# A long-convolution kernel on one Trainium2 core: giving K and X of the product stage PSUM tiles of their own, shared by two units

## The chip, the core and the metric

The kernel runs on one core of a Trainium2 chip. The engines that matter are PE (TensorE, matmuls; its weight loads are shown as PEld), DVE (VectorE), ACT (ScalarE), POOL (GpSimd) and SP, which issues DMAs. The metric is the device time of one execution in microseconds (us).

## The reference

Two blocks follow each other on a sequence of S = 2048 tokens of D = 512 channels. The first is a gated long convolution of `k` and `v`, the second a dense layer with ReLU.

```python
k_shift = sum over t of k_pad[:, t:t+S, :] * shift_k[:, ks-1-t]      # ks = 4 taps
kv  = k_shift * v
y   = irfft(rfft(kv padded to 2S) * rfft(ssm_k padded to 2S))[:S]    # per channel
y   = y + kv * ssm_D
h   = x + layernorm(x) * y                                           # x = A_q
out = h + relu(layernorm(h) @ w1) @ w2
```

The product of the two spectra is what the changed part computes.

## The kernel before, in words

The Fourier transform is done with matmuls in two steps, and so is its inverse. Stage 1 (line 312) transforms the convolution kernel `ssm_k` into the tile BK and the sequence `kv` into the tile BX. BK and BX hold 32 values of a first frequency index, called k1 below, for all 512 channels. The **product stage** (lines 444 to 524) makes the second transform step for each k1 and multiplies the two spectra. Inverse step 1 (line 610, tiles `psi`) follows, then for each quarter of the tokens inverse step 2 (line 701, `pz`), the gate (line 687) and the two matmuls of the dense layer (lines 713 and 729).

The product stage works in eight chunks of four k1. Each chunk has six **units**: u0 to u3, one for each k1 (weights from the table `st`), and s0 and s1, each for two k1 (weights from the table `smc`, which holds sums and differences that give the product by three real multiplications). A unit needs K (from BK) and X (from BX). The four matmuls of one **step** are two for each of two row halves (partitions 0 to 63 and 64 to 127); the halves run at the same time on the two halves of the PE array, so they come in concurrent pairs. A step has 256 columns. For u units K is a step and X is a step. In s units both halves add into the same PSUM banks, so K and X take two steps each (way 1 and way 2): way 1 has the halves write different banks, way 2 swaps the banks, and before way 2 PE waits until its own way 1 has ended (the `nop` with the added dependency, line 484).

PSUM has eight banks. `bank2` (line 151) takes a tile of two banks of 512 words, so four tiles exist at a time (pool `psF`, `bufs=4`). A new tile gets the buffer that was freed first in program order. In the kernel before, a unit has one tile: the first 256 words of each bank hold K, the second 256 hold X. `forms` (line 449) lets ACT copy the K half (2 x 256 words) to SBUF, into `ktu` or `kts`, two buffers each. `times` (line 501) lets DVE multiply X, read from PSUM, by that copy. The product of a u unit overwrites BK at its k1; that of an s unit goes into BXs, the first 32 columns of BX's tile, behind what is still to be read.

The engines run their instructions in the order in which the program has them. For the product stage this order is written out by hand in two strings, FIRST for the first chunk and OTHER for the rest (lines 506 and 507). In them `u0K` is the K step of u0, `s0X2` the second X step of s0, `+u0` an early copy of K, and `=u0` the product, with the copy ahead of it if it wasn't made early:

```python
FIRST = "u0K +u0 u1K +u1 s0K1 s0X1 u0X s0K2 =u0 u1X =u1 s0X2 =s0 s1K1 s1X1 u3K s1K2 s1X2 =s1 u2K u3X =u3 u2X =u2"
OTHER = "s0K1 s0X1 u0K u0X s0K2 u1K =u0 s0X2 =s0 s1K1 s1X1 u1X =u1 s1K2 s1X2 =s1 u3K u3X u2K =u3 u2X =u2"
```

After each chunk POOL makes the table for the chunk three later (`sum_tables`, line 409), and after three of them it adds rows of `w1` (`add_chunks`, line 442) for the column means (line 533), two tiles `pm` of four matmuls in all, which follow the stage on PE. After the stage `w1` is centered by DVE (line 596), ACT copies the second `pm` tile (line 633), POOL and SP begin the work on `x`, and inverse step 1 begins with two `psi` tiles.

Of the kernel before, what the change touches and what calls it, by code (L numbers as in the profile page):

```python
# [9 lines left out]
ALU = mybir.AluOpType  # L10
BF16 = mybir.dt.bfloat16
F32 = mybir.dt.float32
# [3 lines left out]
P = 128  # L16
# [40 lines left out]
def kernel(  # L57
# [13 lines left out]
    nc = tc.nc  # L71
# [9 lines left out]
    halves = (lo, hi)  # L81
# [9 lines left out]
    early = pl.push("early", side="right")  # L91
# [5 lines left out]
    BK = bkp.tile([P, 2, 32, 32, DC * 2], F32R, tag="K", name="BK")  # L97
# [53 lines left out]
    def bank2(name):  # L151
        return psum.tile([P, 2, 512], F32, tag="ps", name=name)[:]
# [69 lines left out]
    st = stp.tile([P, 32, 192], F32R, name="st")  # L222
# [178 lines left out]
    smc = skp.tile([P, 3, 2, 4, P], F32R, name="smc")  # L401
# [3 lines left out]
    def sum_tables(c):  # L405
        ks = slice(4 * c, 4 * c + 4)
        for dp, pq in enumerate(halves):
            for i, op in ((0, ALU.subtract), (1, ALU.add)):
                nc.gpsimd.tensor_tensor(out=smc[pq, c % 3, i, :, 64 * dp:64 * dp + 64], in0=st[pq, ks, 64:128].bitcast(F32),  # L409
                                        in1=st[pq, ks, 0:64].bitcast(F32), op=op)  # L410
# [12 lines left out]
    BX = BXt[:, :, 2:66, :].rearrange("p g (i k) x -> p i g k x", i=2)  # L423
    BXs = BXt[:, :, 0:32, :]
# [7 lines left out]
    prod = pl.push("prod", side="right")  # L432
# [7 lines left out]
    def add_chunks(step):  # L440
        o, a, b = ((wsum, w1[:, 0, :], w1[:, 1, :]), (wpair, w1[:, 2, :], w1[:, 3, :]), (wsum, wsum.bitcast(F32), wpair.bitcast(F32)))[step]
        nc.gpsimd.tensor_tensor(out=o, in0=a, in1=b, op=ALU.add)

    def cols(B, pq, k1, i):
        return B[pq, i].rearrange("p (u w) (v s) x -> p u w v (s x)", w=2, s=2)[:, :, k1 % 2, k1 // 2, :]

    def forms(ps, tag):
        kt = prod.tile([P, 2, 256], F32, tag=tag, name=tag, bufs=2)
        nc.scalar.copy(out=kt[:], in_=ps)  # L449
        return kt  # L450


    def pairs(k1):

        ps = bank2("u")
        begun = []

        def do(what):
            x = "KX".index(what[0])
            for i in range(2):  # L460
                t = st[:, k1, 64:192] if i == 0 else st[:, k1, 0:128]
                for dp, pq in enumerate(halves):
                    nc.tensor.matmul(out=ps[:, dp, 256 * x:256 * x + 256], lhsT=t[pq], rhs=cols((BK, BX)[x], pq, k1, i),  # L463
                                     start=not begun, stop=(i == 1), tile_position=(64 * dp, 0), skip_group_check=True)
                begun.append(i)
        return do, ps, "ktu", BK[:, :, :, k1, :]

    def sums(k1):

        ps = bank2("us")  # L470
        begun = []
        ways = {}

        def do(what):
            x, way = "KX".index(what[0]), int(what[1])
            last = {}
            for i in range(2):
                for dp, pq in enumerate(halves):
                    k = k1 + (dp + way - 1) % 2
                    if i == 0 and dp == 0 and (3 - way, dp) in ways:  # L480

                        turn = nc.tensor.nop()
                        for d in range(2):
                            tc.add_manual_dep(turn.ins, ways[3 - way, d], mybir.DependencyInfo(mybir.DependencyClass.Sync, mybir.DependencyReason.DATA))
                    mm = nc.tensor.matmul(out=ps[:, k % 2, 256 * x:256 * x + 256], lhsT=smc[pq, k // 4 % 3, i, k % 4, :],  # L485
                                     rhs=cols((BK, BX)[x], pq, k, i), start=not begun, stop=(i == 1 and what in begun),
                                     tile_position=(64 * dp, 0), skip_group_check=True)
                    last[dp] = mm.ins.name
                begun.extend((what[0] + "12"[2 - way], i))
            for dp in range(2):  # L490
                ways[way, dp] = last[dp]
        return do, ps, "kts", BXs[:, :, k1:k1 + 2, :].rearrange("p g k x -> p k g x")

    def copy_k(unit):
        do, ps, tag, o = unit
        return forms(ps[:, :, 0:256], tag)

    def times(unit, kt=None):
        do, ps, tag, o = unit
        kt = copy_k(unit) if kt is None else kt  # L500
        nc.vector.tensor_tensor(out=o, in0=ps[:, :, 256:512].rearrange("p b (g x) -> p b g x", x=8),  # L501
                                in1=kt[:].rearrange("p b (g x) -> p b g x", x=8), op=ALU.mult)

    FIRST = "u0K +u0 u1K +u1 s0K1 s0X1 u0X s0K2 =u0 u1X =u1 s0X2 =s0 s1K1 s1X1 u3K s1K2 s1X2 =s1 u2K u3X =u3 u2X =u2"
    OTHER = "s0K1 s0X1 u0K u0X s0K2 u1K =u0 s0X2 =s0 s1K1 s1X1 u1X =u1 s1K2 s1X2 =s1 u3K u3X u2K =u3 u2X =u2"
    for c in range(8):
        units, early = {}, {}
        for step in (OTHER if c else FIRST).split():  # L510
            if step[0] == "+":
                early[step[1:]] = copy_k(units[step[1:]])
                continue
            if step[0] == "=":
                times(units[step[1:]], early.pop(step[1:], None))
                continue
            u = step[:2]
            if u not in units:
                units[u] = (pairs if u[0] == "u" else sums)(4 * c + (1 if u[0] == "u" else 2) * int(u[1]))
            units[u][0](step[2:])  # L520
        if c + 3 < 8:
            sum_tables(c + 3)
        if c in (2, 4, 5):
            add_chunks(max(c - 3, 0))
# [28 lines left out]
    st = late.tile([P, 4, 6], F32, name="st")  # L553
# [260 lines left out]
```

## Time and profile before

| what | value |
|---|---|
| median of 3 runs | 205.06 us (204.96 to 205.13) |
| the profiled execution | 205.23 us; its span, first to last instruction, 203.1 us |
| mean granted clock of TensorE | 0.997 |
| PE busy | 194.7 us, 96% of the span |
| DVE, ACT, POOL busy | 140.3, 115.1, 79.3 us |
| product stage, first matmul to first column mean | 47.63 to 82.43 us |
| one copy of K at line 449, 512 columns | 0.59 us (median) |
| one product at line 501, 512 columns | 0.68 us (median) |

The profile page gives the busy time of each engine, the span in 40 slices, the DMA queues, the chain of work that ended last, and groups of instructions by line. The trace behind it can be asked for the waits of each engine, for busy time in stretches of time, and for the instructions in order of time. PE is busy nearly all of the span, but a busy PE is not one that works at its peak: a matmul whose weights come late is recorded as a longer matmul.

### The profile page before, as it was taken

Reading aid. Unit: us, or ns where it says so; the run is one execution under the profiler, and the core shown is the slowest. Engines: PE = TensorE matmul, PEld = TensorE weight load, DVE = VectorE, ACT = ScalarE, POOL = GpSimd, SP = SyncE. Lnnn points to the kernel's source line nnn. Section 1 sums busy time; section 2 is a strip of 40 time slices with the busy share of each in tenths; the row PEclk is TensorE's granted clock in tenths of the full one; section 3 lists DMA queues with packets and bytes.
Section 4 is the critical chain, followed back from the end, with each engine's and each line's share of the span. In section 5 each row is a group of like instructions: output and inputs, shape, how many; then the busy total and the mean of one; then the engine's idle time right before and its main releaser. Section 6 shows DMA issues by size and latency. Waiting matters only on the chain.

```text
span 203.1 us, 4751 instructions
## 1 busy us (share of the span) xinstructions
PE 194.7 (96%) x1929; PEld 136.9 (67%) x1929; DVE 140.3 (69%) x252; ACT 115.1 (57%) x198; POOL 79.3 (39%) x127
## 2 busy tenths in 40 slices
PE   8899899999999999999999999999999999999991
PEld 2565556988899999899998744475445744444460
DVE  4999988796899989997561968994298560360130
ACT  4986785898688777685980188206930174036200
POOL 7979998960569994302003032062002200002000
PEclk9999999999999999999999999999999999999998
DMA  5999990003400000151736999999734705110011
GB/s 190 330 181 226 170 163 3 3 5 91 190 3 0 3 3 0 46 135 29 107 102 203 183 210 213 177 154 94 88 65 97 138 13 103 35 57 14 0 52 52
DMA packets 47300, 19.94 MB, mean 98 GB/s; under 512 B 42186, under 2 KB 45744, under 8 KB 47280
## 3 DMA queue, kind: packets, MB, share of 16 engines
q1 hardware_dynamic: 43616, 16.14, 41.9%
q10 hardware_dynamic: 3664, 3.51, 6.0%
q8 instruction: 15, 0.25, 0.6%
q14 instruction: 5, 0.04, 0.1%
HBM read 7.02 MB, written 2.10 MB: 45 GB/s over the span
## 4 chain that ended last, share of the span: by engine, by line
PE 73%; DVE 1%; ACT 0%; issue 0%
PE ps1m L713 19%; PE ps2m L729 19%; PE psi L610 11%; PE us L485 9%; PE pz L701 7%; PE u L463 7%; PE pm L533 1%; DVE BX L280 0%; DVE BX L501 0%; ACT kts L449 0%; DVE M L731 0%; DVE ax L280 0%
## 5 line engine op out<-in xcount | busy, mean ns | idle before, releaser
L715 ACT ACTIVATE M<-ps1m 128x512 bf16<-128x512 f32 (+1 forms) x44 | 25.1, 595 | 49.4 <-PE ps1m L713 39.0
L729 PE MATMUL ps2m<-M 128*128 128x512 bf16 (+3 forms) x187 | 38.7, 366 | 0.0
L729 PEld LDWEIGHTS <-M 128*128 128x128 bf16 (+1 forms) x187 | 18.2, 98 | 19.9
L713 PEld LDWEIGHTS <-w 128*128 128x128 bf16 (+1 forms) x176 | 17.4, 100 | 19.9
L572 POOL TENSOR_SCALAR rstd<-mv 128x4 f32<-128x4 f32 x8 | 2.2, 276 | 70.2 <-DVE mv L570 70.2
L409 POOL TENSOR_TENSOR smc<-st 64x256 fp32r<-64x256 f32 x32 | 22.8, 731 | 11.2 <-PE us L485 10.3
L731 DVE SCALAR_TENSOR_TENSOR M<-ps2m,rstd,M 128x512 bf16<-128x512 f32 (+1 forms) x13 | 9.2, 707 | 24.2 <-PE ps2m L729 15.7
L501 DVE TENSOR_TENSOR BK<-u,ktu 128x512 fp32r<-128x512 f32 x32 | 21.2, 685 | 3.8 <-ACT ktu L449 3.5
L610 PE MATMUL psi<-inv,BK 128*128 128x128 f32 x128 | 21.1, 255 | 0.0
L449 ACT COPY ktu<-u 128x512 f32<-128x512 f32 x32 | 18.1, 600 | 5.3 <-PE u L463 4.4
L610 PE MATMUL psi<-inv,BX 128*128 128x256 f32 x64 | 20.5, 338 | 0.0
L610 PEld LDWEIGHTS psi<-inv,BK 128*128 128x128 f32 x128 | 19.7, 197 | 0.0
L713 PE MATMUL ps1m<-M,w 128*128 128x512 bf16 (+1 forms) x88 | 19.3, 379 | 0.0
L713 PE MATMUL ps1m<-xT,w 128*128 128x512 bf16 (+1 forms) x88 | 19.3, 379 | 0.0
L485 PE MATMUL us<-BK,smc 64*128 64x256 f32 x128 | 14.4, 300 | 0.4 <-DVE BX L280 0.4
L463 PE MATMUL u<-BK,st 64*128 64x256 f32 x128 | 13.6, 290 | 0.3 <-DVE BX L501 0.2
L485 PE MATMUL us<-BX,smc 64*128 64x256 f32 x128 | 13.3, 281 | 0.0
L463 PE MATMUL u<-BX,st 64*128 64x256 f32 x128 | 13.1, 283 | 0.0
L278 ACT CAST BK<-ps 128x512 fp32r<-128x512 f32 x16 | 9.1, 587 | 6.4 <-PE ps L312 4.4
L610 PEld LDWEIGHTS psi<-inv,BX 128*128 128x128 f32 x64 | 12.1, 196 | 0.3 <-DVE BK L501 0.3
L568 DVE BATCH_NORM_STATS2 st<-M 128x6 f32<-128x512 bf16 x20 | 12.3, 677 | 0.0
L687 DVE TENSOR_TENSOR qT<-pz,qT 128x2048 bf16<-128x2048 f32 x2 | 4.6, 2290 | 10.6 <-DMA qT<-M 6.5
(132 smaller groups left out, 411.6 us busy)
## 6 DMA issues: line engine op xcount, KB each, us to landing
E<-in_A_ssm_k_dram SPq DMA_DIRECT2D x1, 2048.0 KB
out_dram<-M ACTq DMA_DIRECT2D x15, 128.0 KB
w<-in_B_w_dram SPq DMA_DIRECT2D x1, 1376.0 KB
M<-in_B_w_dram ACTq DMA_DIRECT2D x1, 1280.0 KB
M<-in_A_q_dram SPq DMA_DIRECT2D x8, 128.0 KB
xh<-in_A_q_dram SPq DMA_DIRECT2D x4, 128.0 KB
xr<-in_A_q_dram SPq DMA_DIRECT2D x4, 128.0 KB
out_dram<-M ACTq DMA_DIRECT2D x2, 64.0 KB
```

Of the source, the lines that this page charges most:

```text
L409: nc.gpsimd.tensor_tensor(out=smc[pq, c % 3, i, :, 64 * dp:64 * dp + 64], in0=st[pq, ks, 64:128].bitcast(F32), in1=st[pq, ks, 0:64].bitcas ...
L449: nc.scalar.copy(out=kt[:], in_=ps)
L463: nc.tensor.matmul(out=ps[:, dp, 256 * x:256 * x + 256], lhsT=t[pq], rhs=cols((BK, BX)[x], pq, k1, i), start=not begun, stop=(i == 1), til ...
L485: mm = nc.tensor.matmul(out=ps[:, k % 2, 256 * x:256 * x + 256], lhsT=smc[pq, k // 4 % 3, i, k % 4, :], rhs=cols((BK, BX)[x], pq, k, i), s ...
L501: nc.vector.tensor_tensor(out=o, in0=ps[:, :, 256:512].rearrange("p b (g x) -> p b g x", x=8), in1=kt[:].rearrange("p b (g x) -> p b g x", ...
L568: nc.vector.bn_stats(out=st[:, i, :], in_=src[:, i, :])
L610: nc.tensor.matmul(out=o if part == 0 else o[:, P * part - P:P * part], lhsT=src[:, g // 2, :, g % 2::2].rearrange("p c r -> p (c r)"), rh ...
L701: nc.tensor.matmul(out=pz[:, i, :, a:a + w, :].rearrange("p (s r) a n -> p s r (a n)", s=2), lhsT=ax[rho][:, n2 // 2, n2 % 2, :], rhs=ecor ...
L713: nc.tensor.matmul(out=ps1[:fsz, :].rearrange("p (i t) -> p i t", i=4), lhsT=w1[:, c, fc * P:fc * P + fsz], rhs=hT[sc][:, :, c, :], start= ...
L715: nc.scalar.activation(out=h1T[:fsz, fc, :], in_=ps1[:fsz, :], func=ACT.Relu)
L729: nc.tensor.matmul(out=ps2, lhsT=h1T[:ksz, fc, i * P:(i + 1) * P], rhs=w2[:ksz, fc, d0:d0 + w], start=(fc == 0), stop=(fc == NFC - 1))
L731: nc.vector.scalar_tensor_tensor(out=o[:, d0:d0 + w], in0=ps2, scalar=rstd2[:, t, :], in1=xh[sc][:, i, d0:d0 + w], op0=ALU.mult, op1=ALU.add)
```

## The change

K and X get PSUM tiles of their own, each of two banks, and each shared by two units: u0 and u1 share a K tile and an X tile, u2 and u3 do, and s0 and s1 do. A chunk still takes six tiles from the pool. In a tile the results of the two units (or, for s, of the two k1 of a bank) are interleaved: runs of 8 words of the one, then of the other, so that a product can read its tile, and write BK or BXs, in longer runs. ACT copies a whole K tile (1024 columns, three buffers of one tag `kt`), and DVE multiplies a whole X tile (1024 columns). s units now pair the k1 differently: step `s0` covers the first k1 of each of the two banks, `s1` the second. PE's wait for itself comes once for K and once for X of a chunk, where the kernel before has it for each s unit. The order strings change: K of u0 and u1 of the next chunk (marked `'`) and its copy come ahead of the last X steps and the last product of a chunk, and the first chunk begins with six K steps.

```diff
-    def pairs(k1):
-        ps = bank2("u")
...
-    def sums(k1):
-        ps = bank2("us")
...
+    tiles = {}
+
+    def step(c, what):
+        x, e = "KX".index(what[2]), int(what[1])
+        key = c, what[0] + str(e // 2), x
+        if key not in tiles:
+            tiles[key] = bank2(what[0] + what[2]), set(), {}
+        ps, begun, ways = tiles[key]
+        pv = ps.rearrange("p b (u s k x) -> p b k u s x", s=2, k=2, x=8)
+        way = int(what[3]) if what[0] == "s" else 1
+        if 3 - way in ways:
+            turn = nc.tensor.nop()
+            for mm in ways.pop(3 - way):
+                tc.add_manual_dep(turn.ins, mm, mybir.DependencyInfo(mybir.DependencyClass.Sync, mybir.DependencyReason.DATA))
+        last = {}
+        for i in range(2):
+            for dp, pq in enumerate(halves):
+                if what[0] == "u":
+                    bank, k = dp, 4 * c + e
+                    t = st[pq, k, 64:192] if i == 0 else st[pq, k, 0:128]
+                else:
+                    bank = (dp + way - 1) % 2
+                    k = 4 * c + e + 2 * bank
+                    t = smc[pq, c % 3, i, k % 4, :]
+                mm = nc.tensor.matmul(out=pv[:, bank, e % 2], lhsT=t, rhs=cols((BK, BX)[x], pq, k, i), start=bank not in begun,
+                                      stop=(i == 1), tile_position=(64 * dp, 0), skip_group_check=True)
+                begun.add(bank)
+                last[dp] = mm.ins.name
+        if what[0] == "s":
+            ways.setdefault(way, []).extend(last.values())
+
+    def copy_k(c, name):
+        kt = prod.tile([P, 2, 512], F32, tag="kt", name="kt", bufs=3)
+        nc.scalar.copy(out=kt[:], in_=tiles[c, name, 0][0])
+        return kt
+
+    def times(c, name, kt):
+        ps = tiles[c, name, 1][0]
+        if name[0] == "u":
+            k = 4 * c + 2 * int(name[1])
+            o = BK[:, :, :, k:k + 2, :].rearrange("p d g k x -> p d g (k x)")
+        else:
+            o = BXs[:, :, 4 * c:4 * c + 4, :].rearrange("p g (b k) x -> p b g (k x)", b=2)
+        nc.vector.tensor_tensor(out=o, in0=ps.rearrange("p b (g y) -> p b g y", y=16), in1=kt[:].rearrange("p b (g y) -> p b g y", y=16), op=ALU.mult)
...
-    FIRST = "u0K +u0 u1K +u1 s0K1 s0X1 u0X s0K2 =u0 u1X =u1 s0X2 =s0 s1K1 s1X1 u3K s1K2 s1X2 =s1 u2K u3X =u3 u2X =u2"
-    OTHER = "s0K1 s0X1 u0K u0X s0K2 u1K =u0 s0X2 =s0 s1K1 s1X1 u1X =u1 s1K2 s1X2 =s1 u3K u3X u2K =u3 u2X =u2"
+    FIRST = "s0K1 s1K1 u0K u1K +u0 s0K2 s1K2 +s0 u0X u1X =u0 s0X1 s1X1 u2K u3K +u1 s0X2 s1X2 =s0 u0K' u1K' +u0' u2X u3X =u1"
+    OTHER = "s0K1 s1K1 u0X u1X s0K2 s1K2 +s0 =u0 s0X1 s1X1 u2K u3K +u1 s0X2 s1X2 =s0 u0K' u1K' +u0' u2X u3X =u1"
```

In the new strings `+u0` and `=u0` stand for the pair u0 and u1, `+u1` and `=u1` for the pair u2 and u3, and `+s0` and `=s0` for both s units. In the prediction a tile is called by its letters, so sK is the K tile of the s units of a chunk, and uK' is the K tile of the next chunk's u0 and u1.

## The prediction

> **What bounds the kernel now.** I read the page first, then the waits and the busy time by stretches of the product stage (47.6 to 84.1 us), then its timeline, since the stage is the only one that the change touches. The page's first part gives each engine's busy time, its share of the span and its instructions; the group rows give busy time and mean ns, then the idle time before and who ended it.
>
> ```profile
> PE 194.7 (96%) x1929; PEld 136.9 (67%) x1929; DVE 140.3 (69%) x252; ACT 115.1 (57%) x198; POOL 79.3 (39%) x127
> L501 DVE TENSOR_TENSOR BK<-u,ktu 128x512 fp32r<-128x512 f32 x32 | 21.2, 685 | 3.8 <-ACT ktu L449 3.5
> ```
>
> TensorE is the bound, and the waits view gives it only 0.2 us of idle time after 84 us: what the product stage ends earlier, the kernel ends earlier. The stage runs from its first matmul (47.63) to the first of the column means (82.43). The stretches below are its first chunk, one in the middle and the last (stretch, length, then busy us of PE, PEld, DVE, ACT, POOL):
>
> ```profile
> 47.63:52.55 4.92, 4.51 (x66) 4.24 (x66) 2.94 (x5) 3.27 (x8) 0.54 (x1) 1.00 0.75 246
> 61.34:65.56 4.22, 4.22 (x66) 4.04 (x65) 3.86 (x7) 3.32 (x7) 4.07 (x4) 1.00 0.00 0
> 78.23:82.43 4.20, 4.20 (x66) 4.03 (x65) 3.86 (x7) 3.30 (x7) 0.04 (x1) 1.00 0.00 0
> ```
>
> PE looks full, but "busy" hides stalls here, because matmuls overlap and one that waits for its weights is recorded as longer. The starts of the steps (four matmuls each, 16 steps a chunk) tell more:
>
> ```profile
> 60.97 0.41 PE L463 MATMUL u<-BX,st 64*128 64x256 f32 x4
> 61.11 0.68 DVE L501 TENSOR_TENSOR BX<-us,kts 128x512 fp32r<-128x512 f32 x1
> 61.34 0.51 PE L485 MATMUL us<-BK,smc 64*128 64x256 f32 x4
> ...
> 61.90 0.46 PE L463 MATMUL u<-BK,st 64*128 64x256 f32 x4
> ...
> 62.19 0.41 PE L463 MATMUL u<-BX,st 64*128 64x256 f32 x4
> ...
> 62.65 0.59 ACT L449 COPY ktu<-u 128x512 f32<-128x512 f32 x1 [0.61 <-PE u L463]
> 62.68 0.41 PE L463 MATMUL u<-BK,st 64*128 64x256 f32 x4
> ```
>
> Undisturbed steps start 0.242 us apart (62.19 and 62.68 have one step between them), 0.121 per pair of concurrent matmuls. Sixteen would take 3.87; a chunk takes 4.22. The missing 0.35 is at the chunk's first step (60.97 to 61.34, a tile that a product still reads), at the next unit (61.90 to 62.19, the same, released by the product that ends at 61.79) and at s1K2 (0.1, TensorE's wait for its own s1X1 one step earlier). DVE has 3.86 busy of 4.22: PE and DVE nearly pace each other. Over the stage: 128 steps x 0.242 = 31.0 of its 34.8 us; 3.8 us are stalls, 1.05 in the first chunk (4.92 - 3.87), 0.69 in the second (4.56, same view), 0.35 in each of the other six.
>
> **The change part by part.** *Matmuls:* the same 512, same weights and moving operands; 30.98 us stay. *Copies:* 48 of 512 columns become 24 of 1024; *products* likewise. The trace has both sizes from PSUM:
>
> ```profile
> L295 ACT COPY xfl<-pst 128x1024 f32<-128x1024 f32 x2 | 2.0, 1024 | 0.7 <-PE pst L291 0.7
> L350 DVE TENSOR_TENSOR E<-pkv,E 128x1024 bf16<-128x1024 f32 x6 | 7.3, 1220 | 1.3 <-PE pkv L347 1.3
> ```
>
> ACT per chunk: 3 x 1.02 = 3.06 instead of 6 x 0.59 (the copy at 62.65) = 3.54. DVE: queued products of 512 start 0.60 apart (two take 1.28 at 82.80, so 1.28 - 0.68), those of 1024 then 0.60 + (1.220 - 0.685) = 1.13; 3 x 1.13 = 3.4 instead of 6 x 0.60 = 3.6. Neither reaches 3.87, so neither is the pace by itself. What counts is which tile comes free late.
>
> *Waits on tiles.* The buffer that was freed first in program order goes to the next tile; the changed program's waits agree. In a steady chunk, counted in pairs (0.121) from its first: sK (pair 0) takes the tile freed by the last chunk's copy +u1, uX (pair 4) that of product =s0, sX (pair 12) that of copy +u0', uK (16) that of =u1, the next uK' (24) that of +s0, uX (28) that of =u0. A step whose last pair starts at j releases its reader 0.28 (one matmul) + 0.04 later (62.60 to 62.65 above). A released PE goes on 0.16 after the product's end: 61.79, and the step after the waiting one at 62.19 instead of 0.242 after its start, so 62.19 - 0.24 - 61.79.
> - =s0: s1X2's last pair is 23, so 2.78 + 0.32 = 3.10; + 1.22 = 4.32; PE may go on at 4.48. The next uX is due at pair 36, 4.36. **Stall 0.12 to 0.14.** As a loop from uX to the next uX: 19 pairs 2.30 + 0.32 + 1.22 + 0.16 = **4.00 us a chunk**, against 4.22.
> - +u1: u3K's last pair 19: 2.30 + 0.32 + 1.02 = 3.64; its semaphore about 0.05 later; the weights of sK are due one pair ahead of it, at 3.75. Slack 0.06, and a loss up to 0.14 beyond it costs nothing, as uX waits right behind.
> - +s0: 1.33 + 0.32 + 1.02 = 2.67; uK' is due at 2.78: slack 0.06. =u0 starts at 1.65 (it may overwrite BK only after s1K2), ends 2.87; due 3.27. =u1 starts 1.13 behind =s0, at 4.23, ends 5.45, which is 1.45 in the next chunk; due 1.82. +u0' ends 4.60, due 5.2.
> - TensorE's own wait before s0K2 and s0X2 now has two steps between: its 0.1 a chunk goes.
>
> *First chunk.* Now it stalls for the last copies of the stage before (chain of waits, start and length):
>
> ```profile
> 48.09 0.61 DVE BX L280
> 48.70 0.14 issue
> 48.83 0.75 PE us L485 x8
> ```
>
> Two steps had run since 47.63, so 48.83 was due at 48.11: 0.7 lost. Afterwards six K steps come before the first that needs BX or these tiles: 47.63 + 6 x 0.242 = 49.08, behind the end of the copies (48.70 on DVE, about 48.82 on ACT). What hides them is the moved K work; nothing is late in its place, since +u0 (48.8 to 49.8) and +s0 (to 50.8) meet their tiles at 49.9 and 50.9, with 0.05 each.
>
> *Tail.* What follows hangs on the last product's end:
>
> ```profile
> 82.80 1.28 DVE L501 TENSOR_TENSOR BK<-u,ktu 128x512 fp32r<-128x512 f32 x2
> ...
> 83.53 1.36 PE L610 MATMUL psi<-inv,BX 128*128 128x256 f32 x8
> 83.99 3.08 DVE L596 TENSOR_TENSOR w<-w,pm 128x1376 bf16<-128x1376 bf16 x2
> ```
>
> It ends at 84.08, and the second psi tile, the centering, the copy of pm, POOL's and SP's first loads of x all start within 0.15 us of it. A product of 1024 makes this tail worse: =u1 has to queue behind =s0.
>
> *Sum.* First uX of chunk 1: =s0 of the first chunk is released by pair 27: 3.27 + 0.32 + 1.22 + 0.16 = 4.97, so 52.60. Six loops of 4.00: 76.60. Last =s0 starts at 76.60 + 2.30 + 0.32 = 79.22, =u1 1.13 later, 80.35, and ends at 81.57. That is 2.5 us ahead of 84.08 (the stalls and products saved give about 2.9, the tail takes 0.4 back). One 0.05 us semaphore instruction on PE and a few near-zero slacks take some: **2.4 us**. POOL is no bound: its table and column sums follow chunk 2 as now and end some 1.2 us sooner than today's 78.3, before the column means at about 79.5. No DMA is added or moved; w1 is issued at 47.63 as now. The profiled execution took 205.23 (span 203.1 and 2.1 around it); 205.23 - 2.4 = 202.8. The runs shown have the median 205.06, so **202.7** in their terms.
>
> *One cost that the trace doesn't show:* results are now written in runs of 8 words with gaps of 8. Nearest row: the stage-1 matmuls (L312) write 128 columns in four runs of 32, and their pairs start 0.055 apart (46.16, 46.22, 46.27 in the timeline). The MLP's matmuls take 9.51 us for 44 of 512 columns, 0.00042 a column, so 128 need 0.054: at most 0.001 for four runs, below 0.0005 a gap (or nothing). 256 columns need 0.108, and the pace here is 0.121 (psi at L610 shows why: there 128 columns take 0.114 each, 16 from 84.73 to 86.56, and 256 take 0.12, so the weights are the limit), so 31 gaps of 0.0005 make 0.124 at most: 0.8 us over the stage if nothing hides it. I take 0, the value of the nearest row, and keep 0.8 for the range. The Trainium skill speaks against the change: PSUM — Partial Sum Buffer, Specifications (TRN2), has 8-byte cachelines there and says that "any non-contiguous AP slows matmuls significantly". It gives no price. By that sentence the sum above would be too low; L312's rows do not agree with it for runs of 32, and no run here shows runs of 8.
>
> **Rivals.**
> - *The product paces more than its row says* (partial gain). For: the loop of 4.00 holds one product in full, and each 0.1 on it costs 7 x 0.1. Against: 512-column products keep to 678 to 693 ns with POOL busy beside them. At 1.40 instead of 1.22: 1.3 us less gain, 204.0.
> - *Gaps cost time, slower.* Price if a run takes as long as the 16 words that it spans: 512 x 0.00042 = 0.215 a pair, 256 x 0.215 = 55.0 instead of 34.8, and 0.4 for the tail: 225.7. It decides from about 0.132 a pair (32 pairs then take today's 4.22), or 0.0008 a gap. Against: L312.
> - *It doesn't do what it says:* K a group ahead brings nothing, because today PE waits for products, not copies. Then only the head and TensorE's own wait are gained (0.7 + 8 x 0.1), the tile waits of today come back elsewhere, and the longer tail (0.4) and the uX stall (0.14 x 7) eat it: 205.0. Against: the waits above, of which only uX comes late.
>
> **How the numbers follow.** Forecast (201.8 to 203.6) 0.73; product paces 0.13; no effect 0.05; gaps 0.09. A measurement of this kernel tells about 0.2% (0.4 us) from no change. Low end: no uX stall at all, another 0.9 gained, 201.8. High end: the 0.8 of the gaps and half of the first rival, 204.2; gaps beyond that and the rest are left out. Faster: 0.73 + 0.12 + 0.01 = 0.86; same 0.04; slower 0.10.
>
> **What would show it.** Right: chunks of 4.00 +- 0.05 us; a stall of uX on the 1024 product and nowhere else above 0.05; no wait between 47.63 and the first uX; products at 1.22 and copies at 1.02; steps 0.242 apart; last product ending 81.4 to 81.9; the rest as long as now. Wrong: steps further apart (gaps), chunks of 4.2 with a longer product, or PE idle time behind 84 us that is not there today.

## The result and the profile after

| what | before | after |
|---|---|---|
| median | 205.09 us (204.91 to 205.20, 6 runs) | 203.01 us (202.78 to 203.68, 6 runs) |
| the profiled execution, and its span | 205.23, 203.1 | 203.68, 201.9 |
| first matmul of the product stage | 47.63 | 48.07 |
| end of the last product, from there | 36.45 | 34.82 |
| end of the last product to the end of the span | 119.0 | 119.0 |

The changed kernel takes 0.9897 of the time before, with an interval of 0.9876 to 0.9919. That is 2.08 us less, where 2.4 were forecast. The product stage accounts for 1.63 of it in the traces, not for 2.5. The page's busy times and its groups for the product, in the columns of the page shown before:

```profile
PE 193.6 (96%) x1921; PEld 136.3 (68%) x1929; DVE 138.0 (68%) x228; ACT 112.5 (56%) x174; POOL 79.4 (39%) x127
L494 DVE TENSOR_TENSOR BK<-uX,kt 128x1024 fp32r<-128x1024 f32 x16 | 19.5, 1219 | 3.2 <-PE sK L475 1.9
L494 DVE TENSOR_TENSOR BX<-sX,kt 128x1024 fp32r<-128x1024 f32 x8 | 9.8, 1224 | 1.9 <-PE sX L475 1.9
```

A product of 1024 columns takes what the row of the same size took in the kernel before (1220 ns). The next view gives the busy time by stretches of the stage; the chunks are the first, the second and one in the middle:

```profile
48.07:52.53 4.46, 4.46 (x73) 4.46 (x74) 2.97 (x4) 4.33 (x7) 0.80 (x2) 1.00 0.73 230
52.53:56.60 4.07, 4.07 (x68) 3.95 (x66) 3.54 (x4) 2.96 (x4) 2.84 (x5) 1.00 0.25 98
64.83:68.94 4.11, 4.11 (x68) 3.96 (x66) 3.58 (x4) 2.96 (x4) 3.96 (x6) 1.00 0.02 4
```

The first chunk has 18 steps now (two of the next chunk's), which need 4.36 at 0.242 each: of 1.05 us of stalls 0.10 are left. A steady chunk takes 4.07 to 4.12 instead of 4.22; 4.00 were forecast. The timeline around one uX step tells where the 0.1 is (start, length, operation, idle time before and its releaser):

```profile
63.38 0.64 PE L475 MATMUL sX<-BX,smc 64*128 64x256 f32 x8
...
64.16 1.23 DVE L494 TENSOR_TENSOR BX<-sX,kt 128x1024 fp32r<-128x1024 f32 x1 [0.26 <-PE sX L475]
...
65.44 0.54 PEld L475 LDWEIGHTS uX<-BX,st 64*128 64x128 f32 x8 [0.15 <-DVE BX L494]
65.44 0.76 PE L475 MATMUL uX<-BX,st 64*128 64x256 f32 x8
...
66.03 0.65 PE L475 MATMUL sK<-BK,smc 64*128 64x256 f32 x8
...
66.72 1.02 ACT L484 COPY kt<-sK 128x1024 f32<-128x1024 f32 x1 [1.15 <-PE sK L475]
```

The last sX matmul ends at 63.38 + 0.64 = 64.02; the product that it releases starts at 64.16, **0.14** later, where 0.04 was forecast. It ends at 65.39 and uX goes on, recorded from 65.44; its second step starts at 65.79, so PE lost 65.79 - 0.24 - 65.39 = 0.16 after the product's end, which is called the restart below. A copy is released faster: sK ends at 66.03 + 0.65 = 66.68, and its copy starts at 66.72, 0.04 later. The single records of the six steady chunks give, for the forecast's loop: uX to the end of s1X2 2.59 (forecast 2.58), hand-over 0.11 to 0.14 (0.04), product 1.22 (1.22), restart 0.16 (0.16); together 4.08 to 4.11. Apart from the two uX steps no step of these chunks starts more than 0.02 late. The first product of the stage shows a short hand-over. There the wait that ends last is the one for the copy, and it stands on the product itself:

```profile
49.41 1.02 ACT L484 COPY kt<-uK 128x1024 f32<-128x1024 f32 x1
...
50.45 1.22 DVE L494 TENSOR_TENSOR BK<-uX,kt 128x1024 fp32r<-128x1024 f32 x1 [1.33 <-ACT kt L484]
```

It starts 0.03 after the copy's end (50.42), although DVE had been idle for 1.33. So the 0.14 is not what an idle DVE needs to start. The end of the stage, same view:

```profile
80.53 1.23 DVE L494 TENSOR_TENSOR BX<-sX,kt 128x1024 fp32r<-128x1024 f32 x1 [0.23 <-PE sX L475]
81.67 1.21 DVE L494 TENSOR_TENSOR BK<-uX,kt 128x1024 fp32r<-128x1024 f32 x1
82.94 0.75 PE L601 MATMUL psi<-inv,BX 128*128 128x256 f32 x4 [0.38 <-DVE BK L494]
83.03 0.11 POOL L555 MEMSET mhalf<- 128x4 f32 x1 [5.24 <-DVE BK L494]
```

The tail is as forecast: from the start of the second last product to the end of the last 2.36 (2.35 forecast). PE waits 0.38 for it, and POOL had been done since 77.79 (83.03 - 5.24).

### The profile page after: what moved, and what is told of

Its sections match the earlier page's. It is cut to its first block, busy times and chain, and to the rows that moved or that the text cites. A ratio compares the mean times of both kernels' runs of the same rounds, so it can differ in the third digit from the quotient of the medians.

```text
span 201.9 us, 4693 instructions
## 1 busy us (share of the span) xinstructions
PE 193.6 (96%) x1921; PEld 136.3 (68%) x1929; DVE 138.0 (68%) x228; ACT 112.5 (56%) x174; POOL 79.4 (39%) x127
## 4 chain that ended last, share of the span: by engine, by line
PE 88%; DVE 9%; issue 1%; ACT 0%; DVEq 0%
PE ps1m L704 19%; PE ps2m L720 19%; PE psi L601 11%; PE pz L692 7%; PE pkv L347 6%; PE ps L312 5%; PE uX L475 5%; PE sK L475 4%; PE uK L475 4%; PE sX L475 4%; DVE BX L280 3%; PE pst L291 2%; PE psz L157 2%; DVE G L227 1%; DVE G L225 1%
## 5 line engine op out<-in xcount | busy, mean ns | idle before, releaser
L706 ACT ACTIVATE M<-ps1m 128x512 bf16<-128x512 f32 (+1 forms) x44 | 25.1, 595 | 49.4 <-PE ps1m L704 39.0
L704 PEld LDWEIGHTS <-w 128*128 128x128 bf16 (+1 forms) x176 | 17.4, 100 | 19.9
L494 DVE TENSOR_TENSOR BK<-uX,kt 128x1024 fp32r<-128x1024 f32 x16 | 19.5, 1219 | 3.2 <-PE sK L475 1.9
L704 PE MATMUL ps1m<-M,w 128*128 128x512 bf16 (+1 forms) x88 | 19.3, 379 | 0.0
L704 PE MATMUL ps1m<-xT,w 128*128 128x512 bf16 (+1 forms) x88 | 19.3, 379 | 0.0
L484 ACT COPY kt<-uK 128x1024 f32<-128x1024 f32 x16 | 15.9, 1015 | 0.1
L278 ACT CAST BK<-ps 128x512 fp32r<-128x512 f32 x16 | 9.2, 586 | 6.7 <-PE ps L312 4.0
L484 ACT COPY kt<-sK 128x1024 f32<-128x1024 f32 x8 | 8.1, 1017 | 8.0 <-PE sK L475 8.0
L475 PE MATMUL uX<-BX,st 64*128 64x256 f32 x128 | 11.2, 293 | 0.0
L494 DVE TENSOR_TENSOR BX<-sX,kt 128x1024 fp32r<-128x1024 f32 x8 | 9.8, 1224 | 1.9 <-PE sX L475 1.9
L325 DVE TENSOR_TENSOR BK<-ps,dmask 128x512 fp32r<-128x512 f32 x16 | 10.5, 681 | 0.7 <-ACT BK L278 0.7
```

Of the source, the lines that this page charges most:

```text
L325: todo.append((lambda o=o, pv=pv, dm=dm: nc.vector.tensor_tensor(out=o[0], in0=pv[0], in1=dm, op=ALU.add), lambda o=o, pv=pv: copy("A", o[ ...
L475: mm = nc.tensor.matmul(out=pv[:, bank, e % 2], lhsT=t, rhs=cols((BK, BX)[x], pq, k, i), start=bank not in begun, stop=(i == 1), tile_posi ...
L484: nc.scalar.copy(out=kt[:], in_=tiles[c, name, 0][0])
L494: nc.vector.tensor_tensor(out=o, in0=ps.rearrange("p b (g y) -> p b g y", y=16), in1=kt[:].rearrange("p b (g y) -> p b g y", y=16), op=ALU ...
L704: nc.tensor.matmul(out=ps1[:fsz, :].rearrange("p (i t) -> p i t", i=4), lhsT=w1[:, c, fc * P:fc * P + fsz], rhs=hT[sc][:, :, c, :], start= ...
L706: nc.scalar.activation(out=h1T[:fsz, fc, :], in_=ps1[:fsz, :], func=ACT.Relu)
```

## The experiments

The line numbers are those of the changed kernel; where a kernel adds a line, later ones move by one or two. "From first matmul to last product" is the stage's length in a kernel's trace, 34.82 in the changed kernel.

**The head alone.** X of u0 and u1 is asked for third in the first chunk, as a kernel would that does not begin with K:

```diff
-    FIRST = "s0K1 s1K1 u0K u1K +u0 s0K2 s1K2 +s0 u0X u1X =u0 s0X1 ...
+    FIRST = "s0K1 s1K1 u0X u1X u0K u1K +u0 s0K2 s1K2 +s0 =u0 s0X1 ...
```

> The changed kernel, but its first chunk asks for the X tile of u0 and u1 in third place, ahead of their K (s0K1 s1K1 u0X u1X u0K u1K). Theory: the change gained about 0.7 us by putting six K steps ahead of everything that needs the last copies of stage 1. Then u0X waits for these copies again, 0.7 to 0.8 us after the second step, and no later chunk changes: 203.0 + 0.75 = 203.75. Rival (the head gained nothing, because the first chunk is limited by its products further on): 203.0.

Measured: 204.26 us (203.86 to 205.91), 0.996 [0.9944, 0.9976]; the first chunk takes 5.57 instead of 4.46. Timeline of its first chunk:

```profile
47.91 0.19 PEld L475 LDWEIGHTS uX<-BX,st 64*128 64x128 f32 x2 [0.22 <-ACT BX L278]
48.40 0.42 PEld L475 LDWEIGHTS uX<-BX,st 64*128 64x128 f32 x6 [0.30 <-ACT BX L278]
...
50.69 0.54 PEld L475 LDWEIGHTS uK<-BK,st 64*128 64x128 f32 x8 [0.40 <-ACT kt L484]
```

The wait for the previous stage's copies (L278) came back with about the 0.7 us that the prediction had read off the kernel before. The expectation missed the last line: K of u0 and u1 now comes two steps later, so its copy ends later too, and so does the tile that it frees for u2K: 0.4 us more. So undoing the head costs 1.1 us of the stage (35.96 instead of 34.82), and the 0.7 of the prediction holds for the first link only.

**K one group ahead, alone.** Its steps go back into their own chunk:

```diff
-    OTHER = "s0K1 s1K1 u0X u1X s0K2 s1K2 +s0 =u0 s0X1 s1X1 u2K u3K +u1 s0X2 s1X2 =s0 u0K' u1K' +u0' u2X u3X =u1"
+    OTHER = "s0K1 s1K1 u0K u1K +u0 s0K2 s1K2 +s0 u0X u1X =u0 s0X1 s1X1 u2K u3K +u1 s0X2 s1X2 =s0 u2X u3X =u1"
```

> The changed kernel without K one group ahead: every chunk has the order of the first one without the primed steps, so K of u0 and u1 and its copy come in their own chunk. Theory: the tile that comes late is then sX's, freed by the last chunk's =u1; the loop is 11 pairs (1.33) to s1X2's last pair, 0.28 + 0.14 until =s0, 1.14 until =u1, 1.22 + 0.16: 4.27 us a chunk against 4.11, 7 x 0.16 = 1.1 more: 204.1. Rival (K ahead brings nothing, the wide tiles alone do it): 203.0.

Measured: 204.23 us (203.93 to 204.40), 0.9956 [0.9944, 0.9968]; steady chunks of 4.25 to 4.30. Busy time by stretches for one chunk, and what PE's weight loads waited for in it:

```profile
64.24:68.49 4.25, 4.14 (x68) 3.93 (x66) 3.57 (x4) 2.92 (x4) 4.10 (x6) 1.00 0.01 4
```
```profile
PEld sX L475 <- DVE BK L494: 0.3, 1, 0.3
```

As expected, the stall moves to s0X1, which waits for u1's product. The large copies and products alone bring nothing in a steady chunk (4.25 to 4.30 against 4.22 before); what is gained there comes from the K steps that are moved. The stage takes 35.98, 1.16 more than in the changed kernel. Together with the 1.14 of the head that is more than the 1.63 that the change gains in the stage, so the two are not shares of it; no run undoes both.

**The hand-over to the product.** The product needs the tile from PE and the copy of K from ACT. In the compiled program it waits for ACT only, and a semaphore instruction of DVE ahead of it waits for PE. Here a copy of one word per partition on DVE waits for ACT ahead of each s product, so that the product itself waits for PE:

```diff
+    seen = consts.tile([P, 1], F32, name="seen")
...
+                if what[1] == "s":
+                    nc.vector.tensor_copy(out=seen[:], in_=kts[cc, what[1:]][:, 0, 0:1])
```

> The changed kernel with one tiny DVE copy (128 x 1, a word of the copied K) ahead of each s product. It takes over the wait for ACT, so that the product itself waits for TensorE alone. Theory: the loop of 4.11 us is 0.10 longer than forecast because a product that waits for two engines starts 0.14 after the last matmul instead of 0.04, a separate semaphore instruction standing ahead of it; then a chunk becomes 4.01 and the kernel 203.0 - 7 x 0.1 = 202.3. Rival (the 0.1 is latency of DVE itself or of its queue): chunks of 4.11 or, with the tiny copy's own 0.06 to 0.15 us on DVE, up to 4.2: 203.0 to 203.6.

Measured: 202.69 us (202.33 to 202.75), 0.9879 [0.9866, 0.9892]; steady chunks of 4.02 to 4.05; the stage takes 34.27 instead of 34.82. Its timeline:

```profile
62.71 0.66 PE L475 MATMUL sX<-BX,smc 64*128 64x256 f32 x8
...
63.15 0.14 DVE L511 COPY seen<-kt 128x1 f32<-128x1 f32 x1
...
63.42 1.23 DVE L494 TENSOR_TENSOR BX<-sX,kt 128x1024 fp32r<-128x1024 f32 x1
```

sX ends at 63.37 and the product starts at 63.42: 0.05 instead of 0.14. An instruction more made the chunk shorter. Two waits as such are not the cause: 21 of the 24 large copies have two as well (for DVE, which frees their buffer, and for PE), and start 0.04 after the matmul. There the semaphore instruction has the wait that was over long before, and the copy itself waits for PE. The first copy of the stage has it the other way, with the late wait for PE on the semaphore instruction, and starts at 49.41, 0.09 after its matmul (49.31). At the product of the changed kernel it is like this too: in the records the semaphore instruction comes first (64.098, 0.021 long), and the product at 64.164. The late wait costs more where it stands on the separate instruction. Nor does the small copy help by keeping DVE awake: the first product of the stage, above, started 0.03 after its release behind 1.33 of idle time.

The changed kernel and this one again, side by side:

> The changed kernel once more, to have it beside e8 in the same runs. Both theories expect 203.0 us (202.8 to 203.7), 0.99 of the kernel before, and steady chunks of 4.07 to 4.12 us.

> The kernel of e3 once more (a tiny DVE copy of one word per partition of the K copy stands ahead of the s product, so that the product itself waits for one engine). Theory (the product that waits for two engines starts 0.10 us late, once in each of seven loops): chunks of 4.03 against 4.10, so 7 x 0.07 = 0.5 us less than e7 in the same runs, 202.5. Rival (the 0.3 us between the medians of e3 and of the changed kernel was the spread of the runs): 203.0, the same as e7 within 0.1.

Measured: 202.94 us (202.84 to 203.41), 0.9905 [0.9888, 0.9921], and 202.63 (202.45 to 202.85), 0.9883 [0.9868, 0.9897]; stages of 34.83 and 34.31. The traces show the same 0.5 us twice, the medians 0.3 (203.01 to 202.69, then 202.94 to 202.63), where 0.7 and 0.5 were expected. The intervals of the two ratios overlap, but over all of these runs the eight with the small copy lie at 202.33 to 202.85 and the ten without at 202.78 to 203.68. It is the fastest version found.

**Products of half the size.** Each product as two of 512 columns; tiles, copies and order stay:

```diff
-        nc.vector.tensor_tensor(out=o, in0=ps.rearrange("p b (g y) -> p b g y", y=16), in1=kt[:]...
+        for b in range(2):
+            nc.vector.tensor_tensor(out=o[:, b], in0=ps.rearrange("p b (g y) -> p b g y", y=16)[:, b], in1=kt[:]...
```

> The changed kernel with each product cut into two of 512 columns, one for each bank; tiles, copies and order stay. Theory: what counts is when the X tile comes free; two queued products end 0.60 + 0.685 = 1.28 after the first one starts instead of 1.225, so a chunk becomes 4.17 and the tail 0.1 longer: 203.0 + 7 x 0.06 + 0.1 = 203.5. Rival (the change gains because half as many products spare DVE their fixed cost): DVE is back at its old count of 48 products and most of the 2 us is lost: 204.5 to 205.

Measured: 204.62 us (204.22 to 205.03), 0.9975 [0.9966, 0.9984]; chunks of 4.22 to 4.27, where 4.17 were expected. Timeline:

```profile
64.00 1.29 DVE L495 TENSOR_TENSOR BX<-sX,kt 128x512 fp32r<-128x512 f32 x2 [0.31 <-PE sX L475]
...
65.40 0.57 PEld L475 LDWEIGHTS uX<-BX,st 64*128 64x128 f32 x8 [0.22 <-PE sK L475]
```

The pair of products takes 1.29, as expected. But the restart of uX, counted as above (second step 65.75, product's end 65.29), is 0.22 instead of 0.16: in this kernel a semaphore instruction of PE ahead of it has the wait for DVE, the late one (65.325, 0.051 long), and the step itself waits for PE; in the changed kernel the step waits for DVE directly. It looks like the cost at the product, on another engine; no run takes it away here. So 4.11 + 0.06 + 0.06 = 4.23. The rival's number came out. Its reason did not: DVE still waits 0.31 for PE ahead of the product, so its amount of work is not the limit. But the account explains the trace and not the whole median: the stage takes 35.94, 1.12 more than in the changed kernel, while the medians differ by 1.61. The traced execution was the fastest of eleven, and where the other 0.5 us lies is open.

**The copy of K behind X.** In the steady chunks of the kernel before, each copy of K stands behind the X step of its unit and waited for it. In the unit u1 this chain closes the loop of 4.22 us (timeline of the kernel before):

```profile
63.65 0.42 PE L463 MATMUL u<-BX,st 64*128 64x256 f32 x4
...
64.11 0.59 ACT L449 COPY ktu<-u 128x512 f32<-128x512 f32 x1
...
64.73 0.69 DVE L501 TENSOR_TENSOR BK<-u,ktu 128x512 fp32r<-128x512 f32 x1
```

X ends at 64.07, the copy at 64.70, the product at 65.42, and the next chunk, whose first tile this product frees, begins at 65.56. This experiment puts that order back: ACT first copies one word of the X tile, and the strings have the K copy right ahead of its product.

```diff
+        nc.scalar.copy(out=seen[:], in_=tiles[c, name, 1][0][:, 0, 0:1])
...
-    OTHER = "s0K1 s1K1 u0X u1X s0K2 s1K2 +s0 =u0 s0X1 s1X1 u2K u3K +u1 s0X2 s1X2 =s0 u0K' u1K' +u0' u2X u3X =u1"
+    OTHER = "s0K1 s1K1 u0X u1X s0K2 s1K2 +u0 =u0 s0X1 s1X1 u2K u3K s0X2 s1X2 +s0 =s0 u0K' u1K' u2X u3X +u1 =u1"
```

> The changed kernel with each K copy put back behind the X steps of its pair, as the copies of the kernel before stood behind X of their unit: ACT first copies one word per partition of the X tile (so it waits for that tile's last matmul), then copies K, and the product follows. Nothing else is left out. Theory (what the change took away is the chain X step, copy, product, which has to fit between two uses of the same tile): the copy of 1.02 us now lies in the loop of every tile, so chunks of 6.0 to 6.5 us instead of 4.1 and 218 to 221 us in all. Rival (ACT has 1 us of slack in a chunk, and where the copies stand costs nothing as long as DVE and PE have the same work): 203 to 205 us.

Measured: 221.31 us (221.26 and 221.36), 1.0772 [1.0629, 1.0915]; steady chunks of 6.4 to 6.5. Timeline of one, and its busy time by stretches:

```profile
68.82 0.16 ACT L485 COPY seen<-uX 128x1 f32<-128x1 f32 x1 [0.90 <-PE uX L476]
68.88 1.02 ACT L486 COPY kt<-uK 128x1024 f32<-128x1024 f32 x1
...
69.93 1.23 DVE L496 TENSOR_TENSOR BK<-uX,kt 128x1024 fp32r<-128x1024 f32 x1 [0.75 <-ACT kt L486]
...
71.20 0.54 PEld L476 LDWEIGHTS uK<-BK,st 64*128 64x128 f32 x8 [0.23 <-DVE BK L496]
```

```profile
67.33:73.79 6.46, 5.36 (x64) 4.26 (x65) 3.67 (x3) 3.22 (x7) 5.70 (x6) 1.00 0.01 3
```

X step, copy, product and the next use of the tile now follow each other, while ACT is busy for 3.22 of 6.46 us. Here tiles shared by two units pay only while the copy is not in that chain: with it, they are 16 us slower than the kernel before, whose copies and products are half as long.

**Gaps in what the matmuls write.** In the product stage a pair of matmuls takes 0.121, and its 256 columns would need 0.108 at the dense layer's pace, so a small cost of the gaps could hide. The 176 matmuls of the first dense layer (L704) are paced by their columns, 512 in 0.216 us. In four kernels they write runs of 8, 4, 2 and 1 words with gaps of the same length, and ACT (L706) reads them back in that order. The edit for 8:

```diff
-  nc.tensor.matmul(out=ps1[:fsz, :].rearrange("p (i t) -> p i t", i=4), ...
+  nc.tensor.matmul(out=ps1[:fsz, :].rearrange("p (u s x) -> p s u x", s=2, x=8), ...
-  nc.scalar.activation(out=h1T[:fsz, fc, :], in_=ps1[:fsz, :], func=ACT.Relu)
+  nc.scalar.activation(out=h1T[:fsz, fc, :].rearrange("p (s u x) -> p s u x", s=2, x=8), in_=ps1[:fsz, :].rearrange("p (u s x) -> p s u x", s=2, x=8), func=ACT.Relu)
```

> The changed kernel with the gaps put where nothing can hide them: the 176 matmuls of the first dense layer have 512 columns each and are paced by their columns (9.51 us for 44, 0.216 each). Here each writes its 512 results in runs of 8 words with gaps of 8 (first the even runs of the bank, then the odd ones), and ACT reads them in that order, so the result is unchanged. Theory (a gap costs nothing): 203.0 us, the dense layer's four blocks of 44 still 9.5 us each. Upper bound of the prediction (0.0005 us a gap, 63 gaps a matmul): 176 x 63 x 0.0005 = 5.5 us more, 208.5. Rival (a run of 8 costs as much as the 16 words that it spans): 176 x 0.216 = 38 us more, 241.

> The same with runs of one word and gaps of one word. Theory (the pace is one column at a time, whatever its address): 203.0 us. Rival (two words that lie side by side are written as one, so single words take two writes): the matmuls of the first dense layer take twice as long, 38 us more, 241; with a loss of some per cent of them, 204 to 206. ACT's reads of single words may add to each of the 44 ReLUs, which PE does not wait for as long as they stay below a block's pace.

> Like e5 and e5b, with runs of 2 words and gaps of 2, after runs of 8 cost nothing (203.04 us) and single words doubled the matmuls' time (240.38 us, 0.43 instead of 0.216 us each). Theory A (words are written in pairs of neighbours, so that a single word costs as much as a pair and a pair nothing more): 203.0 us. Theory B (they are written in fours): a run of 2 costs as much as 4, the matmuls of the first dense layer take twice as long, 240 us; as by theory C (in eights).

> The same with runs of 4 words and gaps of 4. Theories A (pairs) and B (fours): 203.0 us. Theory C (eights): 240 us.

| run and gap, words | median, us | ratio to before |
|---|---|---|
| 8 | 203.04 (4 runs) | 0.9901 [0.9886, 0.9916] |
| 4 | 202.81 (2 runs) | 0.9892 [0.9863, 0.9921] |
| 2 | 203.03 (2 runs) | 0.9903 [0.9866, 0.9939] |
| 1 | 240.38 (4 runs) | 1.1727 [1.1709, 1.1744] |

Half of the layer's matmuls in the groups, with runs of 2 words, then with single words:

```profile
L704 PE MATMUL ps1m<-xT,w 128*128 128x512 bf16 (+1 forms) x88 | 19.3, 379 | 0.0
```
```profile
L704 PE MATMUL ps1m<-xT,w 128*128 128x512 bf16 (+1 forms) x88 | 38.1, 633 | 0.0
```

Runs of two words or more cost nothing; single words double the time (19.3 to 38.1 for 88 matmuls, 0.22 to 0.43 each), while ACT's reads take 0.597 us (median), as without gaps. Of the theories only A, that words are written in pairs of neighbours, fits all four runs; the writing itself is not in the trace. The Trainium skill (PSUM — Partial Sum Buffer, Specifications (TRN2)) has cachelines of 8 bytes there, which agrees, since a pair is 8 bytes. The Trainium skill's "any non-contiguous AP slows matmuls significantly" in the same table does not agree with the runs of 8, 4 and 2 words (202.81 to 203.04 us, 203.01 without gaps). The Trainium skill (Advanced Engine Details and Errata, PSUM Cachelines) also says that every two consecutive elements should be contiguous for best throughput, and with that all four runs agree.

**Where the rest of the 2.08 is.** The kernel before, once more:

> The kernel before once more, for a second trace of it. Its median is 2.08 us above that of the changed kernel, but from the first matmul of the product stage to the end of the last product the traces differ by 1.63 only (36.45 and 34.82), and what follows takes the same. The rest would lie ahead of the stage. The first matmul of the stage came at 47.63 in the one trace of the kernel before and at 47.15 to 48.07 in those of the changed kernel and its variants, which do the same work up to there. Theory (spread from run to run, nothing of the change): the stage of 36.45 +- 0.1 again, its start anywhere from 47.1 to 48.1. Rival (the change lets the stage start earlier): a start at 47.6 or later.

Measured: 204.77 us, span 202.6; stage from 47.16 to 83.59, 36.43 again. So the start of the stage varies from run to run: 47.16 and 47.63 in the two traces of the kernel before, 47.15 to 48.07 in those of the changed kernel and its variants. The traces show no earlier start by the change. What does differ is the time outside the span, from the start of the execution to the first recorded instruction and from the last one to the end: 2.12 to 2.24 us in every one of more than 30 executions of the kernel before, 1.76 to 1.88 in every one of some 60 of the changed kernel and its variants. The medians, 2.19 and 1.82, differ by **0.37**. So 1.63 + 0.37 = 2.00 of the 2.08.

## Why the prediction was right, and where it was not

The median of 203.01 is 0.3 us above the forecast of 202.7 and well inside the range. The mechanism was right, but the closeness is partly luck: the stage was forecast 0.9 us too short, and 0.37 us came from a place that the sum held constant.

- *Matmuls and gaps:* right. Steps start 0.242 us apart in the kernel before and 0.244 in the changed one (medians of all steps; the two starts that the prediction names give 0.245), and the gap runs show that the cost taken as 0 is 0 also where nothing hides it. The bound of 0.8 and the rival of 225.7 are out; a doubling like that rival's was measured only for single words, in the dense layer.
- *Copies and products:* right, 1.015 and 1.22 us (1.02 and 1.22 forecast). The rival of a slower product is out.
- *The loop of 4.00:* **the step that failed.** It put the release of a reader at "0.28 (one matmul) + 0.04". The 0.04 came from a copy (62.60 to 62.65), which waits for PE itself. For the product a semaphore instruction ahead of it does, and it starts 0.11 to 0.14 after the matmul. The loop contains this once a chunk, so 4.08 to 4.11 instead of 4.00. The sum pays it eight times, from the first chunk (0.10) to the last: in the records 0.68 us more than eight times 0.04, of the 0.88 by which the stage is longer than forecast (34.82 against 81.57 - 47.63 = 33.94). The rest is the stage's first step (0.31 instead of 0.24) and hundredths in each loop. The small copy ahead of the product takes 0.5 back and so shows the cause.
- *The stall of uX, and nothing else:* right in place, 0.2 instead of 0.12 to 0.14 in size. Slacks of 0.05 held: no copy came too late.
- *TensorE's own wait, 0.1 a chunk:* it is gone, but was no part of the sum, which goes by the loop. By the trace it could not have been added to it: the chunk of before is a loop too, closed by u1 (its lines stand with the copy of K behind X). TensorE's own wait comes at s1K2, behind X of u1, where PE would only have waited longer for that product. No run removes it alone; the kernel without K a group ahead has lost it too, and its chunks are no shorter than those of before. The rival that took this and the head as the whole gain (205.0) is out: without K a group ahead 204.23 was measured, and with it 203.01.
- *Head:* right. PE runs from 48.07 to the first uX at 49.60 without a wait for the stage before.
- *Tail:* right, 2.36 us for the last two products.
- *The sum:* 2.5 in the stage was 1.63. The 2.1 around the span were taken as fixed and became 1.8. Why is open: the variant with products of 512 has as many DVE instructions as before and also 1.82, the one of 221 us has 1.86, so it depends neither on those nor on the length of the stage.

## What to carry to other kernels

When a buffer's reader closes the loop that paces a stage, look which of its waits stands on the instruction itself and which on a semaphore instruction ahead of it: the wait that ends last belongs on the instruction, and a tiny instruction ahead of it, on the same engine, can take over the wait that ends early (0.07 to 0.1 us a hand-over here). Keep the copy of one operand out of the chain that starts with the other: in this kernel the shared tiles shortened the steady chunks only with the operand that has to be copied a group ahead. An execution's time outside its span belongs in the sum too, and should be compared between kernels before a small difference is put down to a stage.

## What the runs showed of the hardware that was not expected

- A DVE product started 0.11 to 0.14 us after the matmul that released it where a separate semaphore instruction waited for that matmul (seven chunks of the changed kernel), and 0.04 to 0.07 after it where the product itself did. On PE the restart after a product was 0.22 us with, and 0.16 without, such an instruction for the late wait.
- Matmul results written in runs of 2, 4 or 8 fp32 words with gaps of the same length took the time of unbroken ones (0.22 us for 512 columns); single words with gaps of one took 0.43.
- The time outside the span was 0.37 us shorter in the changed kernel and in all its variants; no run tells why.
